# Retention attention and a squared-ReLU feed-forward on one core: shared PSUM banks, permuted q rows, one evacuation per bank

## The chip, the core and the metric

The kernel runs on one NeuronCore of a Trainium2 chip. The core has a matrix engine (TensorE, "PE" in the profile; "PEld" is its loading of the stationary operand), VectorE ("DVE"), ScalarE ("ACT"), GpSimd ("POOL") and SyncE ("SP"), which here only issues transfers. Matrix products land in PSUM, a small memory of eight banks of 512 fp32 columns on each of 128 partitions. Everything else is in SBUF. Sixteen DMA engines move data between HBM and SBUF.

The metric is the time of one execution on the device, in microseconds. Before the change it is 290.94 us (median of three runs, 290.92 to 291.03). The profiled execution spans 289.1 us, at the full TensorE clock throughout.

## What is computed

For each of 8 batches and 8 heads, a causal attention without softmax, with a decay per head; then, for each of the 4608 tokens, a feed-forward of two matrices:

```python
batch, n_heads, seq, head_dim = (8, 8, 576, 64)
scores = scale * np.matmul(q, k.transpose(0, 1, 3, 2))
gamma = 1.0 - 2.0 ** (-5.0 - np.arange(H))
Dmat = np.where(rel >= 0, gamma[:, None, None] ** rel[None, :, :], 0.0)
ret = np.matmul(scores * Dmat, v)

x = ret.transpose(0, 2, 1, 3).reshape(B * S, H * D)      # 4608 x 512
h = x @ w_in                                             # 512 x 2048
g = np.maximum(h, 0.0) ** 2
out = g @ w_out                                          # 2048 x 512
```

All inputs and the output are fp32. The feed-forward is most of the arithmetic.

## The kernel before

The 576 positions of a batch are cut into four chunks of 128 and a tail of 64. A unit is one chunk of one batch (or two tails); there are 36 units in 18 groups of two. In a unit, the work of the eight heads is done in 64-by-64 products that use a quarter of TensorE each, four at a time: scores (`psc`), sums of k times v for the running state R (`psS`), and outputs (`psO`). The decay gamma^(i-j) is split into a factor on v (at the cast), a factor on the output (`gam_full`) and a decay of the state per chunk. VectorE masks the scores out of PSUM into `rT` and multiplies the outputs into `xT`, which is the feed-forward's transposed input.

The feed-forward makes `ph` = w_in times xT, ScalarE applies ReLU (`rl`), ScalarE or VectorE squares (`gT`), and w_out follows. From the third group on, the second matrix is applied by Strassen's scheme in seven products instead of eight, for which VectorE makes four sums (`gS`) of parts of gT, each in two halves.

The whole order of instructions comes from a small list scheduler in Python. Every task has an engine, a key, a duration that the author wrote down, dependences, and counted resources that it acquires and that other tasks free. The scheduler simulates the engines and then emits the tasks in the order in which they started. It decides nothing but the order; the waits on the chip are set by the data.

```python
ps_ff  = tile_pool(name="ps_ff",  bufs=4, space=PSUM)     # ph, po, psT, some psS: one bank each
ps_ret = tile_pool(name="ps_ret", bufs=1, space=PSUM)     # two tags, prS and prO: two banks each
sched = Schedule(dict(ff=4, prS=1, prO=1, g=3, ld=5, wst=4, kq=7, v16=7, rT=4, x=3, ...))

# constants at the start, on GpSimd, before everything below
mask = const.tile([P, 64], FP32); nc.gpsimd.memset(mask, 1.0); 2 x nc.gpsimd.affine_select(...)
mask2 = ...; 4 x nc.gpsimd.affine_select(...)
# later on GpSimd: iota_pt, from which VectorE makes vdl_tail

# a load: 128 positions x 8 heads x 64, rows of 256 bytes
nc.sync.dma_start(out=x, in_=src[b, :, c * P:(c + 1) * P, :].rearrange("h p d -> p h d"))
loaded[name, u] = dma_task(0, 1.2 if loaded else 2.1, fn, ...)
# ... casts to fp16 on GpSimd, then one DMA transpose of k and q: kqT
```

The scores and their masking, the outputs and their evacuation:

```python
def emit_scores(g):
    tile_of["psc", g] = ps_ret.tile([P, 2, 512], FP32, name="psc", tag="prS")
    for s, u in enumerate(units_of(g)):
        kT = tile_of["kqT", u]
        ps = tile_of["psc", g][:, :, cols(s)].rearrange("p a (n i) -> p a n i", i=64)
        for hp in range(NP):
            for a, c in ((0, 0), (1, 1), (0, 1), (1, 0)):
                quad(ps[half(c), a, hp, :], kT[half(a), hp, half(c)], kT[half(a), NP + hp, half(c)], a, c)

def fm(s=s, u=u):                     # one per unit: reads both banks
    nc.vector.tensor_tensor(out=r, in0=tile_of["psc", g][:, :, cols(s)]..., in1=mask..., op=ALU.mult)

def fx(s=s, at=at, u=u):              # one per unit: reads both banks
    nc.vector.tensor_tensor(out=tile_of["x", g][:, :, s * P:(s + 1) * P]...,
                            in0=tile_of["psO", g][:, :, cols(at)]..., in1=gam[units[u][0]], op=ALU.mult)
```

From the eighth group on two tasks of small products per group are joined: `f1` makes the first outputs of group g and the scores of group g+1, and `f2` makes the sums of group g+1 and the other outputs of group g:

```python
def f1():
    emit_out1(g)
    emit_scores(g + 1)
def f2():
    emit_sums(g + 1, "prS")
    if not full_of(g + 1):
        first_waits.append(tile_of["masking", g + 1])
    emit_out2(g)
```

And the sums for Strassen's scheme, with the duration that the scheduler counts for each half:

```python
nc.vector.tensor_tensor(out=Sx(k, h), in0=in0(h), in1=in1(h), op=op)
out_.append(add("DVE", key + h, 0.55, f, deps=deps(h)))
```

Of the kernel before, what the change touches and what calls it, by code (L numbers as in the profile page):

```python
# [9 lines left out]
FP32 = mybir.dt.float32  # L10
# [93 lines left out]
def kernel(  # L104
# [48 lines left out]
    ps_ff = ctx.enter_context(tc.tile_pool(name="ps_ff", bufs=4, space=bass.MemoryType.PSUM))  # L153
    ps_ret = ctx.enter_context(tc.tile_pool(name="ps_ret", bufs=1, space=bass.MemoryType.PSUM))
# [42 lines left out]
    heads = [(4 * n + 2 * a + b, n, a, b) for n in range(2) for a in range(2) for b in range(2)]  # L197
    lncol = const.tile([P, NP], FP32, name="lncol")
    lnrow_R = const.tile([P, NP], FP32, name="lnrow_R")
    for h, n, a, b in heads:  # L200
        nc.vector.memset(lncol[64 * b:64 * b + 64, 2 * n + a:2 * n + a + 1], lng[h])
        nc.vector.memset(lnrow_R[64 * a:64 * a + 64, 2 * n + b:2 * n + b + 1], lng[h])

    mask = const.tile([P, 64], FP32, name="mask")
    nc.gpsimd.memset(mask, 1.0)
    for c in range(2):
        nc.gpsimd.affine_select(out=mask[c * 64:(c + 1) * 64], in_=mask[c * 64:(c + 1) * 64],  # L207
                                compare_op=ALU.is_ge, fill=0.0, base=0, pattern=[[1, 64]], channel_multiplier=-1)
# [9 lines left out]
    for hp in range(NP):  # L218
        nc.scalar.activation(out=gam_f[:, hp, :], in_=iota_f, func=ACTF.Exp, scale=lncol[:, hp:hp + 1])
    gam = {"full": gam_f.rearrange("p n (c i) -> p c n i", c=2),  # L220
           "tail": gam_f[:, :, 0:64].rearrange("p n (c i) -> p c n i", c=1).to_broadcast([P, 2, NP, 64])}
# [7 lines left out]
    SPREAD = 0.1  # L229
    SQ_LATE = (1, 4, 6)  # L230
# [4 lines left out]
    SHARED = ()  # L235
    FIRST = ["k0", "q0", "v0", "k2", "q2", "v2", "w0", "w1", "w2", "w3", "w4", "w5", "w6", "w7", "k4", "q4", "v4", "k6", "q6", "v6"]
    sched = Schedule(dict(ff=4, prS=1, prO=1, g=3, ld=5, wst=4, kq=7, v16=7, rT=4, x=3, rl=3, o=4, p1=2, u2=2, u4=2,
# [6 lines left out]
    warm_ps = []  # L244

# [17 lines left out]
    def make_tail_pool():  # L263
        iota_pt = tile_of["iota_pt"] = const.tile([P, 1], FP32, name="iota_pt")
        nc.gpsimd.tensor_copy(out=iota_pt[0:64], in_=iota_p[0:64])
        nc.gpsimd.tensor_scalar(out=iota_pt[64:128], in0=iota_p[64:128], scalar1=-64.0, scalar2=None, op0=ALU.add)
    tail_pool = add_gated("POOL", 4, "v", 2.2, make_tail_pool)
# [14 lines left out]
    def add_load(u):  # L282
        kind, b, c = units[u]
        for n, (name, src) in enumerate((("k", k), ("q", q), ("v", v))):
            def fn(name=name, src=src):
                x = ld.tile([P, H, D], FP32, name=f"{name}32", tag=f"{name}32")
                tile_of[name + "32", u] = x
                if kind == "full":
# [5 lines left out]
            loaded[name, u] = dma_task(0, 1.2 if loaded else 2.1, fn, acq=("ld",) if n == 0 else ())  # L294
# [58 lines left out]
    def add_unit(u, base):  # L353
# [4 lines left out]
        def sorted_cast(op, out_, in_):  # L358
            op(out=out_.rearrange("p (n b a d) -> p n b a d", n=2, b=2, a=2),  # L359
               in_=in_.rearrange("p (n a b) d -> p n b a d", n=2, a=2))  # L360
# [5 lines left out]
        def fq():  # L366
            sorted_cast(nc.gpsimd.tensor_copy, tile_of["kq", u][:, 1], tile_of["q32", u])
# [19 lines left out]
    def add_unit_pair(u, base):  # L387
# [4 lines left out]
        for i, name in enumerate("kqv"):  # L392
            xs[name] = []
            for e in range(2):
# [3 lines left out]
                def fc(name=name, e=e, eng=eng):  # L398
# [8 lines left out]
                    else:  # L407
                        engines[eng](out=t.rearrange("p (n b a d) -> p n b a d", n=2, b=2, a=2),
                                     in_=x.rearrange("p (n a b) d -> p n b a d", n=2, a=2))
# [42 lines left out]
    def add_ret_pair(g):  # L452
# [7 lines left out]
        for e in range(2):  # L460
            tag = "prS" if e == 0 else "prO"

            def fs(e=e, tag=tag):
                ps = rT["ps", e] = ps_ret.tile([P, 2, 512], FP32, name="psc", tag=tag)
                rT[e] = cast.tile([P, 2, NP, P], FP16, name="rx", tag="kq16")
                for hp in range(NP):
                    for a, s in ((0, 0), (1, 1), (0, 1), (1, 0)):
                        quad(ps[half(s), a, hp * P:(hp + 1) * P], kqT(s)[half(a), hp, half(e)], kqT(s)[half(a), NP + hp, :],
                             a, s)
            t = add("PE", base + 3 + e, 0.4, fs, deps=T["kqT", u] + T["kqT", u + 1], acq=(tag, "kq"))  # L470
            ms = []
            for a in range(2):
                def fm(e=e, a=a):
                    nc.vector.tensor_tensor(
                        out=rT[e][:, a], in0=rT["ps", e][:, a].rearrange("p (n i) -> p n i", i=P),
                        in1=mask2[:, e].rearrange("p (o e) i -> p o (e i)", o=1).to_broadcast([P, NP, P]), op=ALU.mult)
                def fc(e=e):
                    nc.scalar.copy(out=rT[e][:, 1], in_=rT["ps", e][:, 1].rearrange("p (n i) -> p n i", i=P))

                def fp(e=e):  # L480
                    nc.gpsimd.tensor_tensor(
                        out=rT[e][:, 1], in0=rT[e][:, 1],
                        in1=mask2[:, e].rearrange("p (o e) i -> p o (e i)", o=1).to_broadcast([P, NP, P]), op=ALU.mult)
                if a and g in SHARED:
# [606 lines left out]
```

## Time and profile before

| what | value |
|---|---|
| time, median of three | 290.94 us |
| span of the profiled execution | 289.1 us |
| TensorE busy | 282.1 us, 98% |
| VectorE, ScalarE, GpSimd busy | 182.4, 188.2, 84.1 us |
| masks of scores (line 682), 28 | 683 ns each |
| outputs into xT (line 736), 28 | 684 ns each |
| sums gS, 128 in two forms (line 928) | 517 and 485 ns each |
| casts of q on GpSimd, 28 | 660 ns each |
| loads of q, 24 of 256 KB | 5.1 us from issue to landing |
| hardware DMA queue, share of 16 engines | 75.3% |

How to read it: a busy time is the sum of an engine's instructions; matmuls overlap in the pipeline, so a TensorE that is 98% busy may still be slower than it could be. A line number stands for a line of the kernel; all small products carry the line of one helper (345). "x48" is a count. A piece of the chain of waits is a stretch of work that nothing but the piece before it held up. Idle time of an engine off that chain costs nothing.

### The profile page before, as it was taken

The page shows a single profiled execution, that of the slowest core. Times are in us where ns is not written, and L with a number is a line of the kernel's source. Part 1 is how long each engine was busy: PE and PEld are TensorE (multiplying, and loading weights), DVE is VectorE, ACT ScalarE, POOL GpSimd, SP SyncE. Part 2 cuts the span into 40 slices and gives each one's busy share as a digit, 9 for nine tenths or more (in the row PEclk, how much of TensorE's full clock was granted, in tenths as well). Part 3 has the DMA queues.
Part 4 walks back from the last instruction along what each step waited for, and adds up shares of the span by engine and source line. Part 5 has one row for each costly group of instructions (what it writes and reads, how often), then busy time and mean ns, then how long its engine had stood idle before and what let it go on. Part 6 is the DMA issues. An engine that isn't in the chain of part 4 may idle for free.

```text
span 289.1 us, 9988 instructions
## 1 busy us (share of the span) xinstructions
PE 282.1 (98%) x4322; PEld 234.3 (81%) x4322; DVE 182.4 (63%) x381; ACT 188.2 (65%) x361; POOL 84.1 (29%) x121
## 2 busy tenths in 40 slices
PE   8999999999999999999999999999999999999994
PEld 3568755788888888888888888888888888888883
DVE  3772368769585657736686857575777775455622
ACT  5459964685757676767756767676767676747830
POOL 5660035443333243342506061505250500000000
PEclk9999999999999999999999999999999999999999
DMA  7999999999999689999788799899995920201004
GB/s 202 274 208 206 249 291 267 219 203 202 221 188 198 153 201 199 217 219 219 154 199 168 172 194 205 163 196 206 225 182 151 181 76 2 75 2 73 2 8 139
DMA packets 139436, 49.94 MB, mean 173 GB/s; under 512 B 118144, under 2 KB 135040, under 8 KB 139392
## 3 DMA queue, kind: packets, MB, share of 16 engines
q1 hardware_dynamic: 134848, 44.84, 75.3%
q0 software_dynamic: 4224, 4.19, 8.8%
q8 instruction: 34, 0.56, 0.8%
q10 hardware_dynamic: 320, 0.26, 0.4%
q14 instruction: 10, 0.08, 0.1%
HBM read 36.70 MB, written 9.44 MB: 160 GB/s over the span
## 4 chain that ended last, share of the span: by engine, by line
PE 91%; DMA 3%; issue 2%; POOL 2%; DVE 0%; POOLq 0%; DVEq 0%
PE ph L859 44%; PE po L951 34%; PE po L899 5%; PE psO L345 4%; DMA w_in<-in_moe_w_in_dram 3%; PE psc L345 2%; PE psS L345 2%; PE psT L423 1%; POOL mask L215 0%; POOL vx L404 0%; POOL w_in L319 0%; DVE o L974 0%; POOL mask L207 0%; DVE p L1003 0%; POOL mask L211 0%
## 5 line engine op out<-in xcount | busy, mean ns | idle before, releaser
L859 PE MATMUL ph<-xT,w_in 128*128 128x256 f16 x1152 | 139.9, 273 | 0.1
L859 PEld LDWEIGHTS <-w_in 128*128 128x128 f16 x1152 | 110.9, 98 | 14.8 <-DMA w_in<-in_moe_w_in_dram 0.3
L867 ACT ACTIVATE rl<-ph 128x512 f16<-128x512 f32 x144 | 84.5, 588 | 52.5 <-PE ph L859 50.9
L877 ACT ACTIVATE gT<-rl 128x512 f16<-128x512 f16 x118 | 74.4, 631 | 3.4
L951 PEld LDWEIGHTS <-gS 128*128 128x128 f16 x512 | 49.8, 98 | 5.9
L951 PE MATMUL po<-wT,gS 128*128 128x256 f16 x384 | 52.1, 273 | 0.0
L928 DVE TENSOR_TENSOR gS<-gT,gS 128x512 f16<-128x512 f16 x64 | 32.8, 517 | 14.2 <-ACT gT L877 13.5
L951 PEld LDWEIGHTS <-gT 128*128 128x128 f16 x384 | 37.1, 98 | 4.5
L928 DVE TENSOR_TENSOR gS<-gT 128x512 f16<-128x512 f16 x64 | 30.9, 485 | 12.6 <-ACT gT L877 12.5
L359 POOL CAST kq<-k 128x512 f16<-128x512 f32 x28 | 18.6, 663 | 61.4 <-DMA k<-in_k_dram 60.2
L951 PE MATMUL po<-w_out,gT 128*128 128x256 f16 x256 | 34.7, 273 | 0.0
L371 POOL TENSOR_TENSOR v<-v,vdec_full 128x512 f16<-128x512 f32 x24 | 25.4, 1057 | 21.9 <-DMA v<-in_v_dram 20.9
L359 POOL CAST kq<-q 128x512 f16<-128x512 f32 x28 | 18.5, 660 | 30.8 <-DMA q<-in_q_dram 30.6
L964 ACT COPY u<-po 128x256 f32<-128x256 f32 x32 | 11.8, 369 | 19.1 <-PE po L951 18.9
L974 DVE TENSOR_TENSOR o<-po,u 128x256 f32<-128x256 f32 x31 | 13.0, 420 | 16.3 <-PE po L951 10.0
L736 DVE TENSOR_TENSOR xT<-psO,gam_full 128x512 f16<-128x512 f32 x28 | 18.1, 684 | 6.3 <-PE psO L345 6.2
L682 DVE TENSOR_TENSOR rT<-psc,mask 128x512 f16<-128x512 f32 x28 | 18.3, 683 | 4.6 <-PE psc L345 4.5
L879 DVE TENSOR_TENSOR gT<-rl 128x512 f16<-128x512 f16 x26 | 12.8, 492 | 12.6 <-ACT rl L867 11.9
L974 DVE TENSOR_TENSOR o<-po,p 128x256 f32<-128x256 f32 x17 | 7.2, 423 | 17.8 <-ACT u L964 8.8
L951 PE MATMUL po<-wT,gT 128*128 128x256 f16 x128 | 16.8, 273 | 0.0
L951 PE MATMUL po<-w_out,gS 128*128 128x256 f16 x128 | 16.8, 273 | 0.0
L899 PE MATMUL po<-w_out,gT 128*128 128x512 f16 x64 | 15.7, 380 | 0.0
(78 smaller groups left out, 224.0 us busy)
## 6 DMA issues: line engine op xcount, KB each, us to landing
out_dram<-o SPq DMA_DIRECT2D x32, 256.0 KB, 3.7
k<-in_k_dram SPq DMA_DIRECT2D x24, 256.0 KB, 4.8
q<-in_q_dram SPq DMA_DIRECT2D x24, 256.0 KB, 5.1
v<-in_v_dram SPq DMA_DIRECT2D x24, 256.0 KB, 4.9
pair<-in_k_dram SPq DMA_DIRECT2D x4, 512.0 KB, 7.0
pair<-in_q_dram SPq DMA_DIRECT2D x4, 512.0 KB, 7.2
pair<-in_v_dram SPq DMA_DIRECT2D x4, 512.0 KB, 7.0
w_in<-in_moe_w_in_dram POOLq DMA_DIRECT2D x4, 512.0 KB, 8.9
```

The costliest lines, as they stand in the source:

```text
L345: t = nc.tensor.matmul(out_, lhsT=lhsT, rhs=rhs, start=start, stop=True, skip_group_check=True, tile_position=(64 * row, 64 * col))
L359: op(out=out_.rearrange("p (n b a d) -> p n b a d", n=2, b=2, a=2), in_=in_.rearrange("p (n a b) d -> p n b a d", n=2, a=2))
L371: nc.gpsimd.tensor_tensor(out=t, in0=tile_of["v32", u], in1=vdec[kind].rearrange("p (h o) -> p h o", o=1).to_broadcast([P, H, D]), op=ALU. ...
L682: tile_of["masking", g] = nc.vector.tensor_tensor(out=r, in0=tile_of["psc", g][:, :, cols(s)].rearrange("p a (n i) -> p a n i", i=64), in1 ...
L736: nc.vector.tensor_tensor(out=tile_of["x", g][:, :, s * P:(s + 1) * P].rearrange("p n (c i) -> p c n i", c=2), in0=tile_of["psO", g][:, :, ...
L859: nc.tensor.matmul(tile_of["ph", g, fb][:, j, :], lhsT=w_in16[:, m, fi * P:(fi + 1) * P], rhs=tile_of["x", g][:, m, :], start=(m == 0), st ...
L867: nc.scalar.activation(out=t, in_=tile_of["ph", g, fb], func=ACTF.Relu)
L877: nc.scalar.activation(out=t, in_=rl, func=ACTF.Square)
L899: nc.tensor.matmul(tile_of["po", u], lhsT=tile_of["g", g][:, fi, s * P:(s + 1) * P], rhs=w_out16[:, fi, :], start=(fi == 0), stop=(fi == N ...
L928: nc.vector.tensor_tensor(out=Sx(k, h), in0=in0(h), in1=in1(h), op=op)
L951: nc.tensor.matmul(tile_of["pb", g, bank], lhsT=left(i), rhs=right[:, i, :], start=(start and i == 0), stop=(i == HF - 1), skip_group_chec ...
L974: nc.vector.tensor_tensor(out=o_tile(u)[:, half * HM:(half + 1) * HM], in0=bank(x), in1=tile_of[name, g], op=ALU.add)
```

## The change

It does four things.

1. All eight PSUM banks are one pool of single banks (`ps_ff`, 8 instead of 4). Scores, sums and outputs take two banks each from it and free each bank as soon as its one reader has run. So the mask and the output evacuation are cut by bank and no longer by unit.
2. For that, the heads are renumbered (head = 4a + 2n + b instead of 4n + 2a + b), so that one operation per bank covers both units with the right decay factors.
3. q of a full unit is loaded so that each partition holds four consecutive positions of two heads, which makes rows of 1 KB in HBM, in four transfers. Its columns are then permuted (position 4r + t stands at block t, place r). Scores and outputs carry the permutation: the products read q in runs of 16, the mask has the permuted form, and the evacuation of the outputs undoes it by reading PSUM with a step. A second mask (`mask_full`) is needed beside that of the tails.
4. The scheduler's numbers: a load of a full q counts 0.8 instead of 1.2; the second halves of the sums of the third group count 1.0 instead of 0.55.

The aim is to let the dense products have banks that the small products do not hold at the time, and to relieve the transfers. The core of the diff:

```diff
-    ps_ff = ctx.enter_context(tc.tile_pool(name="ps_ff", bufs=4, space=bass.MemoryType.PSUM))
-    ps_ret = ctx.enter_context(tc.tile_pool(name="ps_ret", bufs=1, space=bass.MemoryType.PSUM))
+    ps_ff = ctx.enter_context(tc.tile_pool(name="ps_ff", bufs=8, space=bass.MemoryType.PSUM))
...
-    heads = [(4 * n + 2 * a + b, n, a, b) for n in range(2) for a in range(2) for b in range(2)]
+    heads = [(4 * a + 2 * n + b, n, a, b) for n in range(2) for a in range(2) for b in range(2)]
...
-    mask = const.tile([P, 64], FP32, name="mask")
-    nc.gpsimd.memset(mask, 1.0)
-    (two affine_selects, pattern=[[1, 64]])
+    mask = {}
+    for kind, pattern in (("tail", [[1, 64]]), ("full", [[1, 4], [4, 16]])):
+        m = mask[kind] = const.tile([P, 64], FP16, name=f"mask_{kind}")
+        nc.gpsimd.memset(m, 1.0)
+        (two affine_selects, pattern=pattern)
...
-    sched = Schedule(dict(ff=4, prS=1, prO=1, ..., rT=4, ...))
+    sched = Schedule(dict(ff=8, prS=1, prO=1, ..., rT=2, ...))
+    def banks(name):
+        return [ps_ff.tile([P, 512], FP32, name=name, tag="ff") for i in range(2)]
...
+                if kind == "full" and name == "q":
+                    for j in range(NP):
+                        nc.sync.dma_start(out=x[32 * j:32 * j + 32].rearrange("r (a t) d -> r a (t d)", a=2),
+                                          in_=src[b, :, c * P:(c + 1) * P, :].rearrange("(a x) (r t) d -> x r a (t d)", a=2, t=4)[j])
...
-            loaded[name, u] = dma_task(0, 1.2 if loaded else 2.1, fn, ...)
+            loaded[name, u] = dma_task(0, QL if name == "q" and kind == "full" else 1.2, fn, ...)     # QL = 0.8
...
+    def qT(u, a, x, c):
+        t = tile_of["kqT", u][half(a), NP:]
+        return t[:, x, half(c)] if units[u][0] == "tail" else t[:, :, 32 * x + 16 * c:32 * x + 16 * c + 16]
...
-                    quad(ps[half(c), a, hp, :], kT[half(a), hp, half(c)], kT[half(a), NP + hp, half(c)], a, c)
+                    quad(ps[a][half(c), hp, :], tile_of["kqT", u][half(a), hp, half(c)], qT(u, a, hp, c), a, c)
...
-        for s, u in enumerate(units_of(g)):       # mask: one per unit
+        for a in range(2):                        # mask: one per bank
-                    out=r, in0=tile_of["psc", g][:, :, cols(s)]..., in1=mask...
+                    out=tile_of["rT", g][:, :, a], in0=tile_of["psc", g][a].rearrange("p (s n i) -> p s n i", s=2, i=64),
+                    in1=mask[units[units_of(g)[0]][0]]...
+            sched.free("ff", [m])
...
+        for c in range(2):                        # outputs: one per bank
+                    out=tile_of["x", g].rearrange("p n (s e i) -> p e (n s) i", s=n, e=2)[:, c],
+                    in0=y.rearrange("p (o t r) -> p o r t", o=n * NP, t=4) if full else y.rearrange("p (o r t) -> p o r t", o=n * NP, t=4),
+                    in1=gam_f[:, :, 64 * c * full:64 * c * full + 64]..., op=ALU.mult)
+            sched.free("ff", [x])
...
             def f2():
-                emit_sums(g + 1, "prS")
-                if not full_of(g + 1):
-                    first_waits.append(tile_of["masking", g + 1])
+                first_waits.append(tile_of["masking", g + 1])
+                emit_sums(g + 1)
                 emit_out2(g)
-            acq=("prO", "prS")
+            acq=("prO", "prS", "ff", "ff", "ff", "ff")
...
-                out_.append(add("DVE", key + h, 0.55, f, deps=deps(h)))
+                out_.append(add("DVE", key + h, BESIDE if g == STRASSEN and h else 0.55, f, deps=deps(h)))   # BESIDE = 1.0
```

The cast of a full q on GpSimd follows the new layout; the paired units at the start (the first eight) keep their loads and their operations and only take their banks from the shared pool.

## The prediction

> **What bounds the kernel now.** I read five views of the profile of before, in this order: the page's busy shares, the waits of TensorE, the groups of instructions, the chain of waits over one group of two units, and the timeline of the start.
>
> The page's first two parts, engine, busy microseconds and share, then forty slices in tenths:
>
> ```profile
> PE 282.1 (98%) x4322; PEld 234.3 (81%) x4322; DVE 182.4 (63%) x381; ACT 188.2 (65%) x361; POOL 84.1 (29%) x121
> ...
> PE   8999999999999999999999999999999999999994
> ```
>
> TensorE is at nine tenths or more in every slice but the first and the last, and no other engine is above two thirds. The view of waits, for TensorE alone (engine, line, releaser, microseconds, times, longest):
>
> ```profile
> PE warm L249 <- DVE wT L164: 1.3, 1, 1.3
> PE psS L345 <- POOL vx L404: 0.5, 1, 0.5
> ```
>
> Both are in the start. So I count TensorE's stream rather than waits. In the page's groups:
>
> ```profile
> L859 PE MATMUL ph<-xT,w_in 128*128 128x256 f16 x1152 | 139.9, 273 | 0.1
> ...
> L951 PE MATMUL po<-wT,gS 128*128 128x256 f16 x384 | 52.1, 273 | 0.0
> ...
> L951 PE MATMUL po<-w_out,gT 128*128 128x256 f16 x256 | 34.7, 273 | 0.0
> ...
> L951 PE MATMUL po<-wT,gT 128*128 128x256 f16 x128 | 16.8, 273 | 0.0
> L951 PE MATMUL po<-w_out,gS 128*128 128x256 f16 x128 | 16.8, 273 | 0.0
> L899 PE MATMUL po<-w_out,gT 128*128 128x512 f16 x64 | 15.7, 380 | 0.0
> ```
>
> The 273 ns are one matmul from end to end, with the next one already under way. The pace is in the chain of waits over one steady group (start, length, piece, count):
>
> ```profile
> 203.49 4.47 PE ph L859 x40
> 207.96 1.75 PE po L951 x16
> 209.71 1.31 PE ph L859 x12
> 211.01 0.44 PE po L951 x4
> 211.45 0.44 PE ph L859 x4
> 211.89 1.31 PE po L951 x12
> ```
>
> 16 in 1.75 us is 109 ns each, and no piece begins later than its forerunner ends. 1152 + 896 matmuls of 256 columns at 109.2 ns are 223.6 us; the 64 of 512 columns run 4 in 0.86 us, 216 ns each, 13.8 us. The first of them starts at 17.74 us; TensorE ends at about 284.0, where the last two additions of the chain begin; the span is 289.1. So 17.7 (start) + 237.4 + 5.1 (last additions and stores) leave 28.9 us for the 64-by-64 work and the transposes in between, which the gaps between first and last matmul of those blocks give too (29 us in the records). Nothing is left over: time can come only from the start, from these 29 us, or from the tail.
>
> [...] the sums of gT and gS take 0.41 to 1.30 us with a median of 0.42 between 120 and 250 us. [...] a 256-byte packet took 22.7 ns on average, a 1 KB packet 66, not 91.
>
> **The change part by part.** I compared the order of instructions in both built programs, engine by engine.
>
> *q in 1 KB rows.* 24 loads of 1024 rows of 256 bytes become four transfers each, 256 rows of 1 KB in all. On 16 engines: 1024 x 22.7 / 16 = 1.45 us before, 256 x 66 / 16 = 1.06 us after, 0.4 us less each, 9.5 us of DMA time less. In return the SyncE queue issues 72 transfers more; the cheapest one in the trace (a store of 128 rows) took it 0.33 us, so four cost at least 1.3 us where one q load took 1.17 on average. Both lie beside TensorE: the transposes of a group were issued 7 to 14 us ahead of its scores. Effect on the end: 0.
>
> *Permuted q.* Same count of score and state products. The cast on GpSimd writes blocks of 64 elements as before (660 ns). Effect: 0.
>
> *One operation per bank.* Two masks of 683 ns and two outputs of 684 ns stay two of 512 elements each[...]. The output's input is read with a step of 16 elements; I allow 50 ns each, since the output of the paired units, whose operands are stepped too (line 573), takes 731 ns in the groups by form. 24 x 0.05 = 1.2 us of VectorE, none of it waited for: between the last output product of a group and its first ph stand 44 to 76 dense matmuls (18 to 64 before), at least 4.8 us.
>
> *Shared banks.* Freed one by one, and eight rather than four for the dense products. A saturated TensorE can gain only what it loses at blocks: three blocks of the same 80 products took 0.855 to 0.870 us where others took 0.925 and 1.002, and one of 64 took 0.862 where its fellows took 0.737. That sums to about 0.4 us; I book half, −0.2. The order has 36 blocks of small products between dense ones where before had 35; the entry into one shows a gap of 0.09 plus one of 0.12 us: +0.2.
>
> *The start.* A second mask of 64 columns is built on GpSimd before the pieces that VectorE waits for:
>
> ```profile
> 2.03 0.15 POOL L205 MEMSET mask<- 128x64 f32 x1
> 2.25 0.52 POOL L207 TENSOR_SCALAR_AFFINE_SELECT mask<-mask 64x64 f32<-64x64 f32 x2
> ...
> 4.63 0.22 POOL L266 TENSOR_SCALAR iota_pt<-iota_p 64x1 f32<-64x1 f32 x1
> ...
> 4.89 0.23 DVE L183 TENSOR_SCALAR vdl_tail<-lnrow,iota_pt 128x8 f32<-128x8 f32 x1 [1.70 <-POOL iota_pt L266]
> 5.03 0.75 DVE L408 CAST kx<-pair 128x512 f16<-128x512 f32 x2
> ...
> 17.74 3.47 PE L859 MATMUL ph<-xT,w_in 128*128 128x256 f16 x28
> ...
> 19.72 1.21 PEld L859 LDWEIGHTS <-w_in 128*128 128x128 f16 x12 [0.34 <-DMA w_in<-in_moe_w_in_dram]
> ```
>
> This is the timeline of the start (start, length, engine, line, operation; in brackets the idle time before it). VectorE sits 1.70 us until GpSimd's iota_pt and only then casts k, which had landed at 4.99 us. 0.15 + 2 x 0.23 = 0.6 us more on GpSimd moves the cast to about 5.6, and with it transposes, scores and the first xT, one after the other; the filler matmuls between them keep their count. The first ph moves from 17.74 to about 18.3. Its 16 matmuls (1.75 us) then end at 20.05 instead of waiting for weights until 19.72: +0.3 us for good.
>
> *Masks among the sums.* In the last six or so joined groups the order on VectorE is now: mask of bank 0, one square, second half of sum 2, two sums, mask of bank 1. Before, both masks stood behind the sums. The product of sum 2's second half stands 20 dense matmuls after the scores. Worked out from the end of the scores: 0.3 us to the mask (as psO to xT in the trace), mask 0.65, square 0.34, sum 0.42 make 1.7 us; 20 x 0.109 = 2.2 us are there. 0.4 us of room, if GpSimd keeps out of it. In before it did not: the square of the group above took 1.09 us and the sum behind it 0.72, with a v operation of GpSimd beside them. GpSimd runs five casts of 0.65 to 1.05 us in 14.5 us, so about every second group is hit, for some 0.2 us past the room: six to nine groups make +0.5 us.
>
> *Group three's sums counted longer* only reorders the first group with sums, whose sums took 0.82 and 1.27 us instead of 0.42; no wait of TensorE stood there before. 0.
>
> Sum: 290.94 − 0.2 + 0.2 + 0.3 + 0.5 = 291.7. The last term is the least sure, and a schedule counting that group longer is one that was tuned against a trace, so I halve it and lean a little further down: 291.3 us.
>
> **The rivals.** First, the shared banks remove more than I see, and the start hides its 0.6 us behind the weights: for it, first weights land when they land; against it, ph began 1.7 us after its xT, held by TensorE's own order. 290.3 to 290.9. Second, VectorE becomes late in every joined group: for it, the 0.4 us of room; against it, 26 us in which the sums waited for ScalarE's squares, time in which a mask can go free. 292 to 294. Third, runs of 16 elements slow TensorE's moving operand: 384 score and about 336 state products read q so, at about 8 ns each in a block; twice that would be +5.8 us, 297. Fourth, transposes come late, since scores stand up to 50 dense matmuls (5.5 us) earlier in the order while loads are cut up: against it, at least 7 us of room before, and the transposes too stand one or two stores earlier in SyncE's order. With it 292 to 293.
>
> **Range and chances.** Gains are capped at about 0.9 us by the sum of TensorE's stream, losses are open: 290.1 to 292.8. Two per cent is 5.8 us. No part can give that; only the third rival can cost it. Faster by over 2%: 0.01, within 2%: 0.95, slower: 0.04.
>
> **What would show it.** TensorE still 98 to 99% busy; the first ph near 18.3 us; ph and po still 109 ns apart, with a gap of a few tenths ahead of the fifth to eighth product of sum 2 in some of the last joined groups; about 8 ns per 64-column product; the output operation at 0.68 to 0.75 us; q's packets a quarter in number. I am wrong if ph starts at 17.7 us still, if these gaps are missing, or if blocks of 48 or 80 small products take over a microsecond.

## The result, and the profile after

The changed kernel takes 292.75 us (median of 4 runs, 292.42 to 293.71), the kernel before 290.93 (290.54 to 291.03): a ratio of 1.0071, interval 1.0045 to 1.0096. It is slower by about 1.8 us, where 0.4 were forecast. In a later comparison the same two kernels stood at 293.07 and 290.64, ratio 1.0086 (1.0070 to 1.0102).

The page's first two parts, busy microseconds by engine and TensorE in forty slices, as before:

```profile
PE 281.2 (97%) x4322; PEld 233.6 (80%) x4322; DVE 179.9 (62%) x381; ACT 187.7 (65%) x361; POOL 85.2 (29%) x124
...
PE   6999999999999999999999999999999999999994
```

TensorE has no more work than before (281.2 us against 282.1); its share fell because the span grew from 289.1 to 290.6. So the loss is waiting, and in forty slices it is too small to be seen. The view of waits shows it (TensorE alone: releaser, microseconds, times, longest):

```profile
PE psT L435 <- DVE kx L420: 1.2, 1, 1.2
PE po L963 <- DVE rT L688: 0.9, 2, 0.6
PE ph L871 <- issue: 0.6, 1, 0.6
PE psS L353 <- POOL vx L416: 0.3, 1, 0.3
```

The first and the last lie in the start. The two in the middle are new, and neither is a data dependency of the algorithm: no product `po` reads a mask `rT`, and "issue" names no releaser at all. The chain over a late steady group shows that the dense stream itself is as it was:

```profile
204.59 4.80 PE ph L871 x44
209.39 1.75 PE po L963 x16
211.14 0.25 PE psO L353 x16
211.39 0.26 PE psc L353 x32
```

44 ph in 4.80 us and 16 po in 1.75 are 109 ns each, as before, and 32 score products, which now read the permuted q, take 0.26 us as they did in the chain of before:

```profile
130.56 0.26 PE psc L345 x32
```

Going through the records of all matmuls of one dense stretch after another and taking off 109.3 ns each (216 for the 512-column ones), I find 2.00 us of standstill in the changed kernel, in three places, and 0.22 us, in one place, in the kernel before ("at" is the start of the matmul ahead of the gap):

```
                 at us    lost us   from -> to                      waits for
before           19.39    0.22      ph -> ph                        weights w_in
after            64.99    0.43      po <- wT,gS -> po <- w_out,gT   mask rT on VectorE
after            94.76    0.79      po <- wT,gS -> po <- w_out,gT   mask rT on VectorE
after           131.82    0.79      ph -> ph                        nothing recorded
```

That is the whole difference in TensorE's stream: without these gaps the last matmul would begin at 286.07 − 2.00 = 284.07 us in the one and 284.54 − 0.22 = 284.32 in the other. Some more lies outside the span: the time exceeds the span by 2.05 to 2.17 us in the ten runs of the changed kernel and by 1.66 to 1.84 in those of the kernel before in the later comparisons. These 0.35 us are counted in every difference below, and nothing here explains them.

**The first two gaps.** The timeline around 64 us (start, length, engine, line, operation; idle time before it in brackets):

```profile
63.55 1.04 POOL L383 TENSOR_TENSOR v<-v,vdec_full 128x512 f16<-128x512 f32 x1 [0.49 <-DMA v<-in_v_dram]
63.60 1.28 DVE L940 TENSOR_TENSOR gS<-gT,gS 128x512 f16<-128x512 f16 x1
...
64.67 0.60 PE L963 MATMUL po<-wT,gS 128*128 128x256 f16 x4
64.80 0.68 DVE L688 TENSOR_TENSOR rT<-psc,mask_full 128x512 f16<-128x512 f32 x1
...
65.53 1.03 PE L963 MATMUL po<-w_out,gT 128*128 128x256 f16 x8 [0.27 <-DVE rT L688]
```

Read it from the bottom. The po at 65.53 opens a new accumulator for product p2. In the order of tiles that was built, this accumulator gets the bank that held a score tile `psc`, and the last reader of that tile is the mask rT, which ends at 65.48. The mask is late because a half sum gS stands before it on VectorE and took 1.28 us instead of the 0.41 it has when alone: GpSimd's v operation runs beside it. (Of the 128 half sums in this profile, 88 have no GpSimd operation beside them and took 0.41 to 0.43 us; the other 40 took 0.41 to 1.29.) In the kernel before, a mask was just as late and held nobody up, since only small products used its bank; the timeline of before at that place:

```profile
64.97 1.04 PE L951 MATMUL po<-w_out,gT 128*128 128x256 f16 x8
...
65.23 0.68 DVE L682 TENSOR_TENSOR rT<-psc,mask 128x512 f16<-128x512 f32 x1
```

Over the whole program, 71 of the 197 dense tiles that take over a used bank now follow a small product that VectorE reads out; before it was 5. Two of the 71 have no slack (0.05 us from the end of the mask to the matmul), the next has 0.79 us.

**The third gap.** The chain at 130 us (start, length, piece):

```profile
130.01 0.87 PE ph L871 x8
130.89 0.38 PE psS L353 x32
131.26 0.40 PE psO L353 x48
131.66 0.43 PE ph L871 x3
132.09 0.63 issue
132.72 0.82 PE ph L871 x6
```

Eighty small products, three dense matmuls, and then nothing. No semaphore wait of that matmul is open, and its weights had been loaded at 131.83. What the trace does have is packets of a queue called "instruction", 34 in all:

```profile
q8 instruction: 34, 0.56, 0.8%
```

(packets, MB, share.) They are 16 KB each. TensorE has 4322 matmuls and 4322 weight loads, 8668 instructions in the trace with its semaphore instructions and drains, and 8668 / 34 = 255. So one packet per 256 instructions (34 x 256 = 8704) is an estimate that fits TensorE's stream. The packets land while TensorE runs, the first at 16.01 us and the last at 284.78. One such packet ran from 130.02 to 131.28 us, and TensorE went on 1.44 us after its end. That was a suspicion, and half of the experiments are about it.

### The profile page after: what moved, and what is told of

Its sections match the earlier page's. It is cut to its first block, busy times and chain, and to the rows that moved or that the text cites. A ratio compares the mean times of both kernels' runs of the same rounds, so it can differ in the third digit from the quotient of the medians.

```text
span 290.6 us, 10112 instructions
## 1 busy us (share of the span) xinstructions
PE 281.2 (97%) x4322; PEld 233.6 (80%) x4322; DVE 179.9 (62%) x381; ACT 187.7 (65%) x361; POOL 85.2 (29%) x124
## 2 busy tenths in 40 slices
DMA packets 122157, 49.94 MB, mean 172 GB/s; under 512 B 94721, under 2 KB 117761, under 8 KB 122113
## 4 chain that ended last, share of the span: by engine, by line
PE 65%; DVE 1%; issue 0%; DVEq 0%
PE ph L871 31%; PE po L963 29%; PE psO L353 3%; PE psS L353 1%; PE psc L353 1%; DVE o L986 0%; DVE rT L688 0%; DVE p L1015 0%; DVEq L986 0%
## 5 line engine op out<-in xcount | busy, mean ns | idle before, releaser
L871 PE MATMUL ph<-xT,w_in 128*128 128x256 f16 x1152 | 138.0, 273 | 0.6 <-issue 0.6
L940 DVE TENSOR_TENSOR gS<-gT,gS 128x512 f16<-128x512 f16 x64 | 31.6, 494 | 20.7 <-ACT gT L889 20.1
L940 DVE TENSOR_TENSOR gS<-gT 128x512 f16<-128x512 f16 x64 | 33.1, 519 | 16.4 <-ACT gT L889 16.4
L367 POOL CAST kq<-k 128x512 f16<-128x512 f32 x28 | 18.0, 644 | 49.1 <-DMA k<-in_k_dram 47.8
L378 POOL CAST kq<-q 128x512 f16<-128x512 f32 x24 | 16.4, 685 | 21.1 <-DMA q<-in_q_dram 21.0
L891 DVE TENSOR_TENSOR gT<-rl 128x512 f16<-128x512 f16 x26 | 11.2, 431 | 13.5 <-ACT rl L879 13.4
L688 DVE TENSOR_TENSOR rT<-psc,mask_full 128x512 f16<-128x512 f32 x24 | 16.1, 682 | 0.5 <-PE psc L353 0.5
```

The lines of the kernel that those rows point to most:

```text
L378: nc.gpsimd.tensor_copy(out=tile_of["kq", u][:, 1].rearrange("p (t a d) -> p a t d", t=4, a=2), in_=tile_of["q32", u].rearrange("p (a t) d ...
L688: tile_of["masking", g] = nc.vector.tensor_tensor(out=tile_of["rT", g][:, :, a], in0=tile_of["psc", g][a].rearrange("p (s n i) -> p s n i" ...
L871: nc.tensor.matmul(tile_of["ph", g, fb][:, j, :], lhsT=w_in16[:, m, fi * P:(fi + 1) * P], rhs=tile_of["x", g][:, m, :], start=(m == 0), st ...
```

## The experiments

All ratios are to the kernel before, run on the same chip in the same comparison (its medians: 290.64 for e1 to e4, 290.70 for e5 to e8, 290.67 for e9 to e12, 290.80 for e13 to e15). Theory A: dense tiles wait for VectorE through the shared banks. Theory D: TensorE's instructions run dry. B and C blame the order on VectorE and q's layout.

**e1, the changed kernel again.** No edit.

> The changed kernel again, as the base of the others. Theory A (dense tiles inherit banks that VectorE reads out late): the two waits of product p2's new po tile on the mask rT, in groups 4 and 6 near 65 and 95 us, stand again, 0.3 to 0.9 us each, because the order of instructions is fixed. Rival D (a shortage of instructions on TensorE, by chance): the third gap near 131.8 us (0.8 us, no releaser) is elsewhere or gone. Time 292.4 to 293.0, ratio to before 1.005 to 1.008.

293.07 us, 1.0086 (1.0070 to 1.0102). The same places again with other sizes: 0.61 us at 65.4 and 0.04 at 95.3 on the mask, 0.41 at 169.8 on the mask as well (a ph this time), and 0.19 at 131.86 behind the very same matmul. Its six runs spread from 292.47 to 294.07, those of before from 290.41 to 291.18; the profiled run was the fastest of the six, so the profile shows less than the median loses. The 80 small products also began 0.2 us late here, at 130.86, 0.1 us after a mask had ended: in the changed kernel `f2` always waits for the mask of the next group, before only for that of the tails (`first_waits` in the diff).

**e2, banks split again.**

```diff
-    ps_ff = ...tile_pool(name="ps_ff", bufs=8, space=PSUM)
+    ps_ff = ...tile_pool(name="ps_ff", bufs=4, space=PSUM)
+    ps_sm = ...tile_pool(name="ps_sm", bufs=4, space=PSUM)   # psc, psS, psO, still freed singly
```

> All of the change but the one pool: dense tiles in four banks of their own, single banks of the small products in the other four. Theory A: no dense tile takes over a bank from a mask, so the waits of po on rT are gone, and the time falls to 290.6 to 291.3 (ratio 0.999 to 1.001). Rival B (VectorE's order with two masks of both units each is what costs): 292.3 to 293. Rival C (q's new layout costs): 292.3 to 293. Rival D: 291.3 to 292 if the third gap stays.

291.67 us, 1.0032 (1.0020 to 1.0044): 1.4 us of the loss gone, 1.0 left. The timeline of e2 at the place of the first gap:

```profile
63.25 1.31 POOL L384 TENSOR_TENSOR v<-v,vdec_full 128x512 f16<-128x512 f32 x1 [0.33 <-DMA v<-in_v_dram]
...
63.57 1.26 DVE L941 TENSOR_TENSOR gS<-gT 128x512 f16<-128x512 f16 x1
...
64.82 0.60 PE L964 MATMUL po<-wT,gS 128*128 128x256 f16 x4
...
65.09 0.68 DVE L689 TENSOR_TENSOR rT<-psc,mask_full 128x512 f16<-128x512 f32 x1
...
65.26 1.04 PE L964 MATMUL po<-w_out,gT 128*128 128x256 f16 x8
```

VectorE is as late as in the changed kernel, GpSimd's v beside a sum of 1.26 us and the mask until 65.77, and p2 starts in the middle of the mask. The delay is the same; what is gone is the bank that passed it on. The third gap, though, is larger (chain of e2):

```profile
130.21 0.40 PE psO L354 x48
130.61 0.65 PE ph L872 x5
131.26 0.78 issue
132.03 1.48 PE ph L872 x12
```

**e3, q as before.**

```diff
-  four loads of 1 KB rows, count 0.8; permuted cast, scores and outputs
+  one load of 256-byte rows, count 1.2; sorted cast, plain order
```

> The shared banks with q as before: one load of rows of 256 bytes, sorted cast, scores and outputs in plain order, counted 1.2 us. Two po tiles of groups 4 and 6 still follow a mask in their bank (the order of instructions up to there is the same), and a third one at a later group. Theory A: 292.2 to 293.2, and the two waits stand. Rival C: 290.9 to 291.4.

291.31 us, 1.0026 (1.0013 to 1.0039). That is the number that rival C had foretold, although the wait at 65.5 us stands (0.32 us). Two things were undone here, the layout and the scheduler's count for a load of q; e7 separates them.

**e4, masks first.**

```diff
-            m = add("DVE", key + a, 0.7, fm, ...)
+            m = add("DVE", -60, 0.7, fm, ...)
```

> The changed kernel with the two masks of a group ahead of everything else that is ready on VectorE, so that the banks of the scores come free earlier than the half sums that stand before them now. The count of dense tiles that follow a small product which VectorE reads stays (78 instead of 71), only the lateness goes. Theory A: the waits on rT fall below 0.2 us in all, but sums of the products come later; 291.0 to 292.0. A rival that says the count of such inheritances costs by itself (a semaphore wait more on each): 292.5 or above. Rival B (masks ahead of sums delay the products that wait for sums): above 292.7, with waits of po on gS.

291.53 us, 1.0033 (1.0021 to 1.0045), and no wait on rT. 78 dense tiles still follow a small product, so it is their lateness that costs, not their number. A wait of 0.27 us of a product on its sum gS appears instead at 78.8. The third gap is missing in this profile too, so the 1.5 us gained on e1 need not be the masks alone.

**e5, the changed kernel shifted by 68 instructions.**

```diff
-        nc.tensor.matmul(warm_ps[0], lhsT=junk[:, 0:P], rhs=junk, ...)
+        for i in range(2):                        # each of the 34 fillers in two halves
+            nc.tensor.matmul(warm_ps[0][:, 256*i:256*i+256], lhsT=junk[:, 0:P], rhs=junk[:, 256*i:256*i+256], ...)
```

> The changed kernel with each of the 34 filler matmuls ahead of the first scores written as two of half the width: the same columns, 34 more weight loads and 34 more matmuls in TensorE's stream, so that everything later stands 68 instructions further on. Theory D (the third gap is TensorE's stream of instructions running dry: the 16 KB refill that the profile shows as an instruction packet begins at 129.4 to 130.0 us, and TensorE stands still after the 48 and 80 small products of group 8 until some 1.45 us after it landed): the refill is asked for 68 instructions earlier, and the gap near 131.8 us is below 0.15 us; the waits of po on rT stay. 292.3 to 292.9 against 293.1 of the changed kernel. Rival (the gap is a hidden wait on another engine or a DMA there): it stays at 0.2 to 0.9 us and the time at 293.1.

291.93 us, 1.0051 (1.0038 to 1.0064): 1.1 us less than e1, more than expected, by nothing but the number of instructions ahead. (Its profile also has less waiting on masks than the two of the changed kernel, 0.56 us against 1.21 and 1.06, and that varies from one execution to the next; so not all of the 1.1 us need be the third gap.) The chain of e5 runs through the place without a piece of "issue":

```profile
130.63 0.37 PE psS L355 x32
131.01 0.40 PE psO L355 x48
131.41 1.64 PE ph L873 x14
```

The waits on the mask stayed (0.35 us at 65.4, 0.21 at 95.1).

**e6, banks split and shifted.** The edits of e2 and e5.

> Banks split again and the instructions shifted: both causes taken away. If theory A and theory D are the whole of it: no gap above 0.3 us in the dense stream beyond the start's, 290.5 to 291.0, ratio 0.999 to 1.001. If something else in the change costs (q's layout, the outputs out of one bank, the order on VectorE): 291.3 or more, as with split banks alone (291.67).

291.24 us, 1.0023 (1.0016 to 1.0031). The span is 289.1 us, that of before, and only the start has a gap (0.51 us, weights). Still the time is 0.5 us over that of before, above the range that I had given. 0.33 us of it lie outside the span: time less span has a median of 2.07 us here and of 1.74 in the runs of before beside it.

**e7, new layout, old count.**

```diff
-    QL = 0.8
+    QL = 1.2
```

> The changed kernel with q's load counted 1.2 us by the scheduler as before, and nothing else changed: the order of tiles in the banks is then that of the run with the old layout of q, so the two differ by the layout alone. Rival C (the layout costs): 0.5 us or more above that run's 291.31. Theory A with D: q's layout costs nothing, 291.0 to 291.6, and what the old layout had seemed to win was the order of small products against the refills and banks.

291.54 us, 1.0025 (1.0014 to 1.0035), the ratio of e3. So the layout costs nothing, and the scheduler's count is worth 1.5 us against e1, 0.27 of them outside the span (1.82 us against 2.09). The wait at 65.7 us is still there (0.72 us).

**e8, masks first and shifted.** The edits of e4 and e5.

> Masks first and instructions shifted. Masks first had no gap of a refill above 0.1 us in its profile, so theory D gives it 0 to 0.4 us in the median: 291.1 to 291.5 against 291.53. If the rest of its loss is waits of products on the sums behind the masks: a wait of po on gS of 0.2 to 0.5 us stays.

291.47 us, 1.0034 (1.0023 to 1.0044): no gain over e4, whose profile had had no gap of that kind. One wait of a po on gS, 0.29 us at 196.4.

**e9, the kernel before, shifted by 40 instructions.** As e5, for 20 of the fillers.

> The kernel before, nothing of the change in it, with 20 of its 34 filler matmuls written as two of half the width: 40 instructions more in TensorE's stream ahead of everything. By the count of instructions this puts the end of group 10's second block of small products (80 of them, with the 48 of its first block only 21 dense matmuls ahead) 8 instructions before the place where the chunk of the next refill is needed, as group 8's stood in the changed kernel. Theory D: a gap of 0.2 to 0.9 us without a releaser appears just after that block, near 160 us, where the kernel before had none; 291.0 to 291.7 against 290.7. Rival (the shift helped the changed kernel by something else, the start for instance): no such gap, 290.4 to 290.9.

290.70 us, 0.9999 (0.9991 to 1.0007), no gap: a miss. The refill at 158.4 us began 31 instructions ahead of the block; in the four profiles that have a gap it was 7 to 23. My count of instructions says where a chunk is needed, not when it is asked for: the packet had landed 1.92 us before its first instruction started, more than the 1.40 to 1.63 us behind which the gaps end.

**e10, shifted, masks first before the joined groups only.**

```diff
-            m = add("DVE", key + a, 0.7, fm, ...)
+            m = add("DVE", -60 if g < JOIN else key + a, 0.7, fm, ...)
```

> The changed kernel, shifted, with the masks ahead of all else on VectorE in the groups before the joined ones alone (two to six). Theory A: the two waits of po on rT are gone and nothing later moves: 0.4 to 0.8 us below the shifted kernel's 291.93, so 291.1 to 291.5. If what masks first had won lay in the joined groups: 291.8 to 292.0.

291.15 us, 1.0021 (1.0013 to 1.0029), 0.8 us below e5, of which 0.3 lie outside the span (time less span is 1.73 us here, 2.03 in e5). Timeline of e10:

```profile
63.57 1.28 DVE L690 TENSOR_TENSOR rT<-psc,mask_full 128x512 f16<-128x512 f32 x2
...
64.77 0.41 DVE L942 TENSOR_TENSOR gS<-gT,gS 128x512 f16<-128x512 f16 x1
```

Both masks are out before the sums, and the two waits at 65 and 95 us are gone. So what masks first wins beside the shift (0.5 us from e5 to e8) lies in these early groups. Two other waits stand in this profile, 0.35 us of a po on its sum gS at 78.6 and 0.30 us of a ph on a mask, through its bank, at 169.2, in a joined group where the masks were not put first.

**e11, shifted, group three's sums counted short.**

```diff
-    BESIDE = 1.0
+    BESIDE = 0.55
```

> The changed kernel, shifted, with the second half sums of group three counted 0.55 us by the scheduler as before. This moves the placement of tiles: the po behind a mask in group 4 comes at the product before, and the one in group 6 is gone. Theory A: what decides is which dense tile follows a mask, not the count by itself: one wait of 0.3 to 1.0 us in group 4, none in group 6, in all 291.7 to 292.4 against 291.93. My prediction gave the count nothing: within 0.3 us of 291.93.

292.41 us, 1.0064 (1.0051 to 1.0076), 0.5 us above e5. One wait on rT of 0.84 us at 65.0, none at 95. The count that I had given nothing is worth half a microsecond here, because it moves which dense tile follows a mask: counted long, the one in group 4 stands four matmuls (0.44 us) later in the stream.

**e12, banks split, q counted 1.2.** The edits of e2 and e7.

> Banks split and q's load counted 1.2 us: q's layout, the output operations out of one bank, the masks of both units and group three's count are what is left of the change, and the blocks of small products lie as in the kernel before, away from the refills. Theories A and D as the whole of it: 290.5 to 291.0, ratio 0.999 to 1.001. If the layout or the new VectorE operations cost by themselves: 291.2 or more.

290.75 us, 1.0002 (0.9994 to 1.0010). q's layout, the output operations out of one bank, the masks of both units and group three's count are all still in it, and it is as fast as the kernel before; rivals B and C fall with it. Its waits of TensorE:

```profile
PE ph L872 <- DMA w_in<-in_moe_w_in_dram: 0.3, 1, 0.3
PE psT L436 <- DVE kx L421: 0.2, 1, 0.2
```

**e13 and e14, shifted by 6 and by 28.** As e5, for 3 and for 14 of the fillers.

> The changed kernel with only 3 fillers in two halves: 6 instructions more. In three runs the gap without a releaser stood at the same place of TensorE's stream, behind the fourth dense matmul after group 8's 80 small products. Theory D: it belongs to a number of instructions and not to an operation, so it moves three matmuls forward in the program, to behind the first dense matmul after the block; its size 0.2 to 0.9 us, time 292.4 to 293.3. Rival (a hidden wait of that operation): it stays behind the fourth.

> The same with 14 fillers in two halves, 28 instructions more. Theory D: the gap moves 14 matmuls forward, into the last ten products of the block itself (psO before psO), 0.1 to 0.9 us, since the refill is also asked for 1.5 us earlier in the stream but needed only some 0.5 us earlier, it is smaller than with 6 more and may be gone: 292.0 to 293.0. Rival: it stays behind the fourth dense matmul.

292.83 us, 1.0077 (1.0062 to 1.0093), and 292.39, 1.0061 (1.0046 to 1.0076). The times fall with the shift, 293.07, 292.83, 292.39 and 291.93 for 0, 6, 28 and 68 instructions. With 6 the profiled run was the fastest of its four (291.88; the others 292.81 to 293.29), and the large gap is in neither profile. What is left of it in e13 stands where theory D puts it: the last small product and the first dense matmul are 0.21 us apart (0.12 or 0.13 behind the 101 other blocks of 80 in the 17 profiles), three matmuls earlier in the program than the gap of the changed kernel and 1.39 us after a packet had landed. In e14 the packet had landed 1.89 us before its first instruction, and nothing stands still. (In these expectations "the fourth" dense matmul is one too many: it is the third, as the chain above shows.)

Clearer is a place that every profile has, the kernel before too. TensorE's first packet lands at 14.2 to 16.3 us, and in 14 of the 17 profiles one of the small products at the start then stands still. The chain of e9 shows it:

```profile
16.92 0.17 PE psc L349
17.09 0.10 issue
17.19 0.64 PE psc L349 x31
```

It is another product in each program, and always the 224th matmul of TensorE's stream (from the packet and matmul records; the last column is the distance from the matmul before, elsewhere in these blocks at most 0.07 us):

```
                        packet landed   it starts   after   it is the         distance
before                  16.03           17.45       1.42    22nd of 32 psc    0.16
shifted by 6 (e13)      16.12           17.45       1.33    19th of 32 psc    0.21
shifted by 28 (e14)     16.11           17.45       1.34     8th of 32 psc    0.23
before, by 40 (e9)      15.84           17.19       1.35     2nd of 32 psc    0.35
shifted by 68 (e8)      14.74           16.18       1.44    28th of 32 psS    0.56
```

In the three profiles without it (e5, e6 and e11) the packet had landed 1.56 to 1.69 us before.

**e15, the kernel before with q counted 0.8 and nothing else.**

```diff
-            loaded[name, u] = dma_task(0, 1.2 if loaded else 2.1, fn, ...)
+            loaded[name, u] = dma_task(0, 0.8 if name == "q" and kind == "full" else 1.2, fn, ...)
```

> The kernel before with nothing but the scheduler's count for a load of q put from 1.2 to 0.8 us, as the change has it; layout, banks and operations are the old ones. The order that comes out puts the end of group 8's 80 small products 10 instructions ahead of a chunk's edge, as in the changed kernel with split banks (that had a gap of 0.94 us there). Theory D: a gap of 0.2 to 1.0 us without a releaser near 131 us, 291.1 to 291.9 against 290.67. Rival (the count is harmless, and the gap needs the new layout's transfers): no gap, 290.5 to 290.9.

291.61 us, 1.0028 (1.0017 to 1.0040). Old banks, old layout, old operations, and the gap is there. Of the 0.81 us that the median loses, 0.36 lie outside the span (2.11 us against 1.75), and this profile has 0.36 us of standstill in the gap. The chain of e15:

```profile
130.53 0.40 PE psO L345 x48
130.93 0.65 PE ph L859 x5
131.58 0.20 issue
131.78 1.27 PE ph L859 x10
```

The four profiles with this gap at its larger size, from the packet and matmul records (the place is the number of TensorE's instruction, weight loads, matmuls and semaphore instructions counted from 0 in the trace):

```
                          refill us        goes on at   after its end   gap lies behind
after                     130.02-131.28    132.72       1.44            no. 4032, 3rd ph after the block
after again (e1)          129.39-130.68    132.15       1.47            no. 4032, 3rd ph
banks split (e2)          129.44-130.40    132.03       1.63            no. 4032, 5th ph
before, q 0.8 (e15)       128.91-130.38    131.78       1.40            no. 4032, 5th ph
```

Three programs, two different matmuls, one number of instructions, and nearly the same time from the end of the packet until TensorE goes on. The first instruction after the standstill is no. 4033 in these four and in e13, and no. 449 at the start, which is 14 x 256 earlier, and in the changed kernel's profile 14 packets earlier. In none of the 17 profiles, over 33 packets each, does an instruction with the number 449 + 256 j start sooner than 1.27 us after its packet has landed. So that TensorE stands still for its instructions I take as shown; what decides when a packet is asked for stays open.

## Why the prediction was wrong

The forecast was 291.3 us in a range of 290.1 to 292.8; the first comparison measured 292.75, the second 293.07. One path through the edits accounts for it (medians; those of before lie within 0.06 us in the comparisons used):

```
changed kernel (e1)                        293.07
  shifted by 68 instructions (e5)          291.93    -1.14   instructions run dry
  and banks split (e6)                     291.24    -0.69   waits on the mask through the banks
  q counted 1.2 instead of shifted (e12)   290.75    -0.49   rest of q's count; 0.33 of it outside the span
kernel before                              290.67
```

The parts depend on the order in which they are taken: splitting first takes 1.40 us, shifting then 0.43. Four runs without the shift show the two parts apart. Against the kernel before, the time rises by 0.08 us with split banks and the old count (e12), by 0.84 with shared banks alone (e7), by 1.03 with the new count alone (e2) and by 2.43 with both (e1), 0.6 more than the two add up to. So two steps of the prediction failed: the value of the shared banks, and the new count, for which it has no term.

- **Shared banks: booked −0.2, cost 0.7 to 1.4 us.** This is the first step that failed. I took a larger pool as a pure gain, capped by what TensorE loses at blocks. A bank carries its last reader with it: a dense tile that used to wait for ScalarE or for a finished addition now waits for whatever VectorE has in its queue. Both halves of the fact were in my text, that VectorE's operations stretch beside GpSimd's v (a square to 1.09 us, a sum to 0.72), and that tiles of both kinds would share banks. I didn't ask, for each dense tile, which operation frees its bank.
- **q in 1 KB rows: 0, by its transfers and its layout.** Right as far as it went, and the second step that failed, by what it left out. The layout costs nothing (e3 against e7, e12): packets under 512 bytes fell from 118,144 to 94,721, and no transpose was late. But the scheduler's count of 0.8 us for the load came with it, and I gave it no term. It is worth 0.9 to 1.5 us in the changed kernel (e12 to e2, e7 to e1) and costs the old one 0.8 us by itself (e15): it moves the blocks of small products against the refills, and 0.3 to 0.4 us of it lie outside the span, for which there is no cause yet. The order of instructions, which I had, showed that these blocks moved; I took that for harmless.
- **Masks among the sums: booked +0.5 in the last six or so joined groups, ahead of the fifth to eighth product of sum 2.** The gaps there are missing in the profile after, one of the signs that I had named for being wrong. Lateness through GpSimd was the right cause, in the wrong place (groups 4 and 6, before the joined ones) and through another wait (a bank, not a sum). Waits on sums came only in variants, 0.2 to 0.35 us in e3, e4, e8, e10 and e12.
- **The start: booked +0.3, not seen.** iota_pt did come later, as worked out: VectorE waited 2.54 us for it instead of 1.70 (timeline of the changed kernel's start). But the first ph starts when it did, at 17.74 us, another of the signs that I had named for being wrong:

```profile
3.05 0.56 POOL L208 TENSOR_SCALAR_AFFINE_SELECT mask_full<-mask_full 64x64 f16<-64x64 f16 x2
...
5.72 0.23 DVE L182 TENSOR_SCALAR vdl_tail<-lnrow,iota_pt 128x8 f32<-128x8 f32 x1 [2.54 <-POOL iota_pt L269]
...
17.74 3.01 PE L871 MATMUL ph<-xT,w_in 128*128 128x256 f16 x26
```

  The transposes waited 1.2 us for the cast, and the scores and fillers behind them took the delay up: the first transposes begin at 6.34 us and before at 5.93, the third set at 12.45 and before at 12.52. The start doesn't repeat well enough for a term of this size: in e1, the same kernel, the first ph is at 18.01, in the other profiles at 17.45 to 17.96.
- **One more block: booked +0.2.** Nothing of it is seen: without its gaps the changed kernel's last matmul would start 0.25 us earlier than that of before.
- **Output operation and permuted q: booked 0 on the path.** Right. The output operation's two forms, after and before (min/median/max ns):

```profile
L747 DVE TENSOR_TENSOR xT<-psO,gam_full x28: 680/681/693, 71.8 to 258.8; 128x512 f16<-128x512 f32 x28
```

```profile
L736 DVE TENSOR_TENSOR xT<-psO,gam_full x28: 672/681/693, 70.6 to 257.2; 128x512 f16<-128x512 f32 x28
```

  The 50 ns that I allowed for the stepped read were not needed. The third rival (runs of 16 elements slow TensorE) is out: 48 products of psO take 0.40 us with permuted q and without (chains of e2 and e15). That the permuted read would cost nothing was an estimate of mine, which no run had shown when I booked it.
- **Group three's longer count: booked 0.** Wrong by 0.5 us, which it saves (e11): in this arrangement it puts the dense tile that follows a mask in group 4 four matmuls later.
- **Leaning down from 291.7 to 291.3**, because the new count looked tuned, halved the only term that stood for a late VectorE, and was the wrong way.
- **A reading that was off.** TensorE does not end at about 284.0 us before: the chain leaves it at 283.95 for the last additions, but its last matmul starts at 284.54. So the remainder of 28.9 us is about half a microsecond too small, which changes none of the terms.

Open: the 0.35 us outside the span (medians of 2.09 us in e1, 2.07 in e6 and 2.11 in e15, where q is counted 0.8, but 1.73 in e10, where it is too; 1.74 in e12 and 1.71 to 1.75 before), and what sets the moment of a refill. Nothing that I ran is measurably faster than the kernel before.

## What to carry to other kernels

When pools are merged, list for each tile of the critical engine which operation frees its slot, and on which engine. With these eight banks in rotation the read-outs mostly overlap with the products (median 3.3 us from the end of a VectorE read-out to the dense matmul that takes the bank), but a rotation that mixes two evacuating engines can make the saturated engine as late as the later of them (0.43 and 0.79 us in the changed kernel). If it waits for a tile that it doesn't read, look for the slot's last reader; the cure is a slot of its own (e2) or an earlier reader (e10). And where a gap on a saturated engine has no releaser, look for an instruction packet before it, and shift the stream by a few instructions: the gap that belongs to a place in the stream then falls on another operation (the 224th matmul above).

## What the runs showed of the hardware

- TensorE's instructions came in while it ran: 34 packets of 16 KB for 8668 instructions, an estimate of 256 to a packet. In the kernels before and after a packet took 0.88 to 1.71 us. The first instruction of a packet, so counted, started 1.27 us after its landing at the earliest (561 packets of 17 profiles), and in the gaps 1.27 to 1.63 us after it. 80 small products used up 160 instructions in some 0.8 us, where dense matmuls at 109 ns take 8.7 us for as many, and it was after such a block that TensorE stood still near 132 us. This gap was 0.09 to 0.94 us, different in each execution.
- A VectorE read of PSUM with a step of 16 fp32 elements cost the same here as a contiguous one: a median of 681 ns for 512 elements a partition either way.
- A moving operand in runs of 32 bytes cost TensorE nothing here: 32 products of 64 columns in 0.26 us either way.
